# A decode step on one core: the query weights in two loads by partitions, and one gather of x

## Chip, cores and metric

The kernel runs on one core of a Trainium2 chip. The metric is device time in microseconds, the median of several executions. Times inside the kernel come from one execution recorded by the hardware profiler; they count from the first instruction (the start of the span).

## What is computed

Two token rows x (B = 2, D = 448, bfloat16) are normalised and go through two branches, attention against a cache and a small feed-forward net, whose results are multiplied:

```python
def reference(A_x, A_k_cache, A_v_cache, A_wq, A_wo, B_x, B_w1, B_w2):
    def _A_ref(x, k_cache, v_cache, wq, wo):          # Hq=16, Hkv=8, Dh=256
        ...
        W = min(4096, max(256, Sk // 4))              # Sk=8192, W=2048: the last 2048 keys
        q = (x @ wq).reshape(B, Sq, Hq, Dh).transpose(0, 2, 1, 3)
        k = jnp.repeat(k_cache[:, :, Sk - W:, :], rep, axis=1)
        v = jnp.repeat(v_cache[:, :, Sk - W:, :], rep, axis=1)
        scores = jnp.einsum("bhqd,bhkd->bhqk", q, k) * (Dh ** -0.5)
        o = jnp.einsum("bhqk,bhkd->bhqd", _softmax(scores, axis=-1), v)
        return o.transpose(0, 2, 1, 3).reshape(B, Sq, Hq * Dh) @ wo
    def _B_ref(x, w1, w2):
        h = jnp.maximum(jnp.einsum("bsd,df->bsf", x, w1), 0)      # Dff=1792
        return jnp.einsum("bsf,fd->bsd", h, w2)
    xn = _layernorm(A_x, axis=-1)
    return A_x + _A_ref(xn, ...) * _silu(_B_ref(xn, B_w1, B_w2))
```

The inputs that weigh are the K and V windows (16.8 MB each), wq and wo (3.67 MB each) and w1 and w2 (1.6 MB each).

## The kernel before

The program lists each engine's instructions by hand (`pr.op`, `pr.dma`), in order, with the instructions each depends on; a helper turns these into semaphore waits. Each engine works through its own list in order. All large loads are issued by SP, one after the other, and stand in one DMA queue. Nearly all matmuls pass through one helper, so the profile puts them on its line, L383, and all DMAs on L46; tile names tell them apart.

The order of SP's loads: wq in two parts (L297, into `wbuf`), then K of quarter 0 and 1 (`kbuf`), V of quarter 0 (`vbuf`), and later, each behind the work that frees its buffer, K of quarter 2 (waits for the transposes of quarter 0), V 1 (for the P·V matmuls of quarter 0), K 3, V 2, then w1 and w2 into `wbuf` (after the q matmuls), V 3, and wo in four parts into `kbuf`. Each quarter of K or V is 4 MB: 128 partitions with 32 KB each.

Work at the start:

- ACT issues two small loads of x (`x_sb`, `x_c`). POOL clears tiles and builds identities and masks, among them `msk` (L303, L304). DVE computes mean and variance (L322, L323), several small mask tiles, the rest of `msk` (L354) and `rstd` (L356).
- `x_rows` (L359) normalises x and spreads it into `xg`; `x_cols` (L366) transposes `xg` into `xt` and multiplies by a mask, which leaves x as columns, seven slots of four columns. Which element of x a partition holds has to fit the way the rows of the weights lie in `wbuf`. A row of wq is taken as two half rows of 2048 columns, 896 half rows in all. In this kernel half rows 0 to 255 go to slots 0 and 1 (two to a partition), half rows 256 to 895 to slots 2 to 6 (five to a partition). The columns for this are `xq` (three row operations, a transpose, four mask multiplications, L377 to L380).
- `do_q` (L386): 28 matmuls of `xq` and `wbuf` into `fbk`; the first eight wait for the first load, the others for the second. DVE scales the result into `qn` and transposes it into `qt`; `do_qbd` (POOL) spreads it into `qbd`.
- A second gather (L542 to L544) puts x into columns in the layout of w1 (seven half rows to a partition), `xr`, which `do_H` uses much later.
- DVE transposes K of quarter 0 (`kt`, L459, four pieces), and PE computes scores from `qbd` and `kt` into `sbk`.

After that the quarters follow each other: maximum, exponential, transpose of the probabilities, P·V into `obk`; the feed-forward net stands before the last quarter's P·V, and the product with wo at the end, in parts as wo lands (`wbk` for the wide columns, `cbk` for the rest).

The listing has the functions that the change touches:

Of the kernel before, what the change touches and what calls it, by code (L numbers as in the profile page):

```python
# [5 lines left out]
BF = mybir.dt.bfloat16  # L6
F32 = mybir.dt.float32
ACT = mybir.ActivationFunctionType
ALU = mybir.AluOpType
AX = mybir.AxisListType  # L10

PE, DVE, ACTE, SP, POOL = "pe", "dve", "act", "sp", "pool"
# [151 lines left out]
def bass_recurrent_scan__sliding_block_cached__dense_activation_relu__decode_kernel(  # L164
# [11 lines left out]
    B, Sq, D = A_x.shape  # L176
# [12 lines left out]
    SLOTS = 7  # L189
    HC = HD // 2  # L190
# [8 lines left out]
    with es:  # L199
        pr = _Prog(nc, es)  # L200

        def named(name, shape, dt):
            return es.enter_context(nc.sbuf_tensor(name, shape, dt))

        def psum(name, shape, dt):
            return es.enter_context(nc.psum_tensor(name, shape, dt))

        def view(t, off, dims, n=128, p0=0, pstep=1):
            width = t.shape[1]
            return bass.AP(t, p0 * width + off, [[width * pstep, n]] + dims)  # L210
# [4 lines left out]
        par8 = named("par8", [128, 8], F32)  # L215
# [8 lines left out]
        x_sb = named("x_sb", [128, D], BF)  # L224
        xg = named("xg", [128, 9 * 128], BF)
        xt = named("xt", [128, SLOTS * 128], BF)
# [2 lines left out]
        sd = named("sd", [128, 3], F32)  # L229
        rstd = named("rstd", [128, 1], F32)  # L230
        xr = named("xr", [128, SLOTS * 4], BF)
        xq = named("xq", [128, SLOTS * 4], BF)
        msk = named("msk", [128, 2 * SLOTS], F32)
        qn = named("qn", [128, 512], BF)
        qt = named("qt", [128, 512], BF)
        qbd = named("qbd", [128, QW], BF)
# [24 lines left out]
        wbuf = named("wbuf", [128, SLOTS * HC], BF)  # L261
# [6 lines left out]
        fbk = psum("fbk", [128, 512], F32)  # L268
# [5 lines left out]
        def kv_src(k, cache):  # L274
            return cache.rearrange("b h s d -> (b h) s d")[k::NQ, SK - W:SK, :].rearrange("g (i t) d -> i g (t d)", t=NT)

        st = {}
        wq_rows = A_wq.rearrange("r (hf c) -> (r hf) c", hf=2)
        wq_src = [wq_rows[0:256, :].rearrange("(p s) c -> p (s c)", s=2),
                  wq_rows[256:896, :].rearrange("(p s) c -> p (s c)", s=5)]  # L280
        w1_src = B_w1.rearrange("r (hf c) -> (r hf) c", hf=2).rearrange("(p s) c -> p (s c)", s=SLOTS)
        w2_src = B_w2.rearrange("(p j) n -> p (j n)", j=14)
        wo_src = A_wo.rearrange("(p j) n -> p (j n)", j=32)
# [2 lines left out]
        def load_k(k):  # L286
            d_k[k] = pr.dma(SP, kbuf[k % 2][:, :], kv_src(k, A_k_cache), [st.get(("T", k - 2, 3))])

        def load_v(k):
# [4 lines left out]
        p_xz = pr.op(POOL, lambda e: e.memset(xg[0:32, :], 0.0))  # L294
        d_xc = pr.dma(ACTE, view(x_c, 0, [[1, NCOL]], n=8, pstep=16),
                      A_x[:, 0, :].rearrange("b (i n) -> i b n", i=4), [p_xc], key="v")
        d_wq = [pr.dma(SP, wbuf[:, lo * HC:hi * HC], src) for lo, hi, src in ((0, 2, wq_src[0]), (2, SLOTS, wq_src[1]))]  # L297
        load_k(0)
        load_k(1)
        load_v(0)  # L300

        i0 = pr.op(POOL, lambda e: e.memset(ident[:, :], 0.0))
        p_m0 = pr.op(POOL, lambda e: e.memset(msk[:, 0:4], 0.0))  # L303
        p_m1 = pr.op(POOL, lambda e: e.memset(view(msk, 0, [[3, 2]]), 1.0), [p_m0])  # L304
        p_id = pr.op(POOL, lambda e: e.affine_select(
            out=ident[:, :], in_=ident[:, :], compare_op=ALU.not_equal, fill=1.0,
            base=0, pattern=[[-1, 128]], channel_multiplier=1), [i0])
# [3 lines left out]
            out=ident_f[:, :], in_=ident_f[:, :], compare_op=ALU.not_equal, fill=1.0,  # L311
            base=0, pattern=[[-1, 128]], channel_multiplier=1), [i1])
        for t0 in (h_sb, h_n, ea, ga):
            p_z = pr.op(POOL, lambda e, t0=t0: e.memset(t0[:, :], 0.0))
        p_one = pr.op(POOL, lambda e: e.memset(one_f[:, :], 1.0))
        p_sz = pr.op(POOL, lambda e: e.memset(sel[:, :], 0.0))

        a_z = [pr.op(ACTE, lambda e, t=t: e.memzero(t[:, :]), key="osb" if t is obk else None)
               for t in (fbk, obk, wbk, cbk)]

        v_xz = p_xz
# [3 lines left out]
            out=sd[0:B, 0:1], in0=st2[0:B, 1:2], scalar1=EPS, scalar2=None, op0=ALU.add), [v_ag])  # L325
# [3 lines left out]
            out=par2[:, :], in_=view(ident, 0, [[1, 2], [2, 64]]), axis=AX.X, op=ALU.add), [p_id])  # L329
        v_par8 = pr.op(DVE, lambda e: e.tensor_copy(  # L330
            view(par8, 0, [[2, 4], [1, 2]]), view(par2, 0, [[0, 4], [1, 2]])), [v_par])
# [3 lines left out]
            out=view(wcol, 0, [[4, 128], [1, 4]], n=4), in0=view(ident, 0, [[0, 128], [1, 4]], n=4),  # L335
            scalar1=1.0, scalar2=BIG, op0=ALU.subtract, op1=ALU.mult))
        v_qm = pr.op(DVE, lambda e: e.tensor_reduce(
            out=qmask[:, :], in_=view(ident, 0, [[32, 4], [1, 32]]), axis=AX.X, op=ALU.add))
# [6 lines left out]
        def fold8_op(e):  # L345
# [4 lines left out]
            view(gsum, 0, [[8, 16], [1, 8]]), view(fold8, 0, [[0, 16], [1, 8]])), [v_f8])  # L350
        v_sz = p_sz
        v_sel = pr.op(DVE, lambda e: e.tensor_copy(view(sel, 0, [[16, 2]]), fold[:, 0:2]), [v_fold, v_sz], key="pt")
        v_m1 = p_m1
        v_m2 = pr.op(DVE, lambda e: e.tensor_copy(  # L354
            view(msk, 4, [[2, 5], [1, 2]]), view(par8, 0, [[1, 5], [1, 2]])), [v_par8])
        v_rs = pr.op(DVE, lambda e: e.reciprocal(rstd[0:B, :], sd[0:B, 1:2]), [a_sd])  # L356
        xs = {"deps": [v_rs, v_xz], "mask": [v_m1, v_m2]}

        def x_rows(lo, blocks, pairs, step, shift, first, behind=False):  # L359
            xs["xn"] = pr.op(DVE, lambda e: e.tensor_scalar(  # L360
                out=view(xg, 128 + 128 * lo + shift, [[256, blocks], [128, 2], [pairs, 128 // pairs]], n=B),
                in0=view(x_sb, first, [[1, blocks], [0, 2], [step, 128 // pairs]], n=B),
                scalar1=st2[0:B, 0:1], scalar2=rstd[0:B, 0:1],
                op0=ALU.subtract, op1=ALU.mult), xs["deps"] + ([xs["xn"]] if behind else []))

        def x_cols(dst, mask):  # L366
            v = pr.op(DVE, lambda e: e.transpose(xt[0:32, :], xg[0:32, 128:128 + SLOTS * 128]),
                      [xs["xn"]] + xs.get("done", []))
            for g in range(4):
                o = pr.op(DVE, lambda e, g=g: e.tensor_tensor(  # L370
                    out=view(dst, 0, [[4, SLOTS], [2, 2], [1, 2]], n=32, p0=32 * g),
                    in0=view(xt, 32 * g, [[128, SLOTS], [1, 2], [0, 2]], n=32),
                    in1=mask, op=ALU.mult), [v, p_one, a_z[-1]] + xs["mask"])
            xs["deps"], xs["done"] = [v], [o]
            return o

        x_rows(2, 3, 2, 5, 0, 128)  # L377
        x_rows(2, 3, 2, 5, -127, 130)
        x_rows(0, 1, 1, 1, 0, 0, True)
        v_xr = x_cols(xq, view(msk, 0, [[2, SLOTS], [0, 2], [1, 2]], n=32))  # L380

        def mm(out_ap, lhsT, rhs, start, stop=False, **kw):
            return lambda e: e.matmul(out_ap, lhsT=lhsT, rhs=rhs, start=start, stop=stop,  # L383
                                      skip_group_check=True, **kw)

        def do_q():  # L386
            deps = [d_wq[0], v_xr]
            for s in range(SLOTS):
                if s == 2:
                    deps = [d_wq[1]]  # L390
                for i in range(4):
                    lo = s * HC + i * 512
                    o = pr.op(PE, mm(fbk[32 * i:32 * i + 4, :], xq[:, 4 * s:4 * s + 4], wbuf[:, lo:lo + 512],
                                     s == 0, s == SLOTS - 1, tile_position=(0, 32 * i)), deps)
                    deps = []
            st["q_mm"] = o
            v = pr.op(DVE, lambda e: e.tensor_scalar(  # L397
                out=view(qn, 0, [[64, 8], [32, 2], [1, 32]]),
                in0=view(fbk, 0, [[64, 8], [1, 2], [2, 32]]),
                scalar1=SCALE, scalar2=None, op0=ALU.mult), [o])  # L400
            st["qT"] = pr.op(DVE, lambda e: e.transpose(qt[:, :], qn[:, :]), [v])
# [7 lines left out]
                deps = []  # L409

        def do_H(u):
            deps = [d_w1, v_xw] if u == 0 else []
            for s in range(SLOTS):
                lo = s * FC + u * (FC // 2)
                o = pr.op(PE, mm((fbk, cbk)[u][0:4, 0:FC // 2], xr[:, 4 * s:4 * s + 4], wbuf[:, lo:lo + FC // 2],
                                 s == 0, s == SLOTS - 1), deps)
                deps = []
            st["h_n"] = pr.op(DVE, lambda e: e.tensor_scalar(
                out=view(h_n, 32 * u, [[64, 14], [1, 32]], n=4), in0=view((fbk, cbk)[u], 0, [[1, 14], [14, 32]], n=4),
                scalar1=0.0, scalar2=None, op0=ALU.max), [o, p_z])  # L420
# [117 lines left out]

        pr.section("PRO", 0)
        do_q()  # L540
        do_qbd(0)
        x_rows(0, 4, 2, SLOTS, -127, 3)  # L542
        x_rows(0, 4, 2, SLOTS, 0, 0)
        v_xw = x_cols(xr, view(par8, 0, [[1, SLOTS], [0, 2], [1, 2]], n=32))  # L544
        for c in range(4):
            do_T(0, c)
        do_S(0, 0)
# [13 lines left out]
        for k in range(1, NQ):  # L561
# [9 lines left out]
            if k == 2:  # L571
                d_w1 = pr.dma(SP, wbuf[:, 0:W2], w1_src, [st["q_mm"]])
# [35 lines left out]
        deps = [st["at", NQ - 1]]  # L608
        for b in range(2):
            m_at = pr.op(PE, mm(mbk[:, 256 + 32 * b:288 + 32 * b], at_exp[:, 128 * b:128 * b + 128],  # L610
                                fold[:, :], b == 0, b == 1), deps)
            deps = []
        keep_busy(sbk, 512)
        v_at2 = pr.op(DVE, lambda e: e.tensor_copy(at2[:, :], mbk[:, 256:320]), [m_at])
        deps = [v_at2]
        for j in range(WO_WIDE):
            i = j % 4
            m_w = pr.op(PE, mm(wbk[32 * i:32 * i + 2, 0:D], view(at2, j, [[32, 2]]), wo_sb[:, j * D:(j + 1) * D],
                               j < 4, j + 4 >= WO_WIDE, tile_position=(0, 32 * i)), deps + [landed.get(j)])
            deps = []  # L620
# [11 lines left out]
        deps = [v_ws]  # L632
        for i in range(4):
            pr.op(PE, mm(cbk[32 * i:32 * i + 17, 0:NCOL], sel[:, :], wsum[:, i * NCOL:(i + 1) * NCOL],
                         True, tile_position=(0, 32 * i)), deps)
            deps = []
        for j in range(WO_WIDE, 32):
# [4 lines left out]
            out=tmp[:, :], in0=cbk[:, 0:NCOL], in1=g_sb[:, :], op=ALU.mult), [m_o, st["g"]])  # L642
        v_o = pr.op(DVE, lambda e: e.tensor_tensor(
            out=out_sb[:, :], in0=tmp[:, :], in1=x_c[:, :], op=ALU.add), [v_t, d_xc])
# [33 lines left out]
```

## Time and profile before

| | |
|---|---|
| median of three runs | 109.77 us (109.68 to 109.82) |
| profiled execution | 109.78 us |
| its span, first to last instruction | 108.5 us |
| PE / PEld / DVE / ACT / POOL busy | 70.5 / 27.2 / 60.5 / 14.9 / 9.0 us |
| mean granted TensorE clock | 0.900 |
| bytes moved, mean rate | 44.13 MB, 407 GB/s |
| issue to landing, first and second part of wq | 4.9 and 10.6 us |

An engine's busy time is no sign of being the bound by itself; what counts is which wait ended last before each step. A time from issue to landing includes the time that a load stands behind others in the queue. KB is 1024 bytes, MB and GB are powers of ten.

### The profile page before, as it was taken

Reading aid. Unit: us, or ns where it says so; the run is one execution under the profiler, and the core shown is the slowest. Engines: PE = TensorE matmul, PEld = TensorE weight load, DVE = VectorE, ACT = ScalarE, POOL = GpSimd, SP = SyncE. Lnnn points to the kernel's source line nnn. Section 1 sums busy time; section 2 is a strip of 40 time slices with the busy share of each in tenths; the row PEclk is TensorE's granted clock in tenths of the full one; section 3 lists DMA queues with packets and bytes.
Section 4 is the critical chain, followed back from the end, with each engine's and each line's share of the span. In section 5 each row is a group of like instructions: output and inputs, shape, how many; then the busy total and the mean of one; then the engine's idle time right before and its main releaser. Section 6 shows DMA issues by size and latency. Waiting matters only on the chain.

```text
span 108.5 us, 1111 instructions
## 1 busy us (share of the span) xinstructions
PE 70.5 (65%) x424; PEld 27.2 (25%) x424; DVE 60.5 (56%) x86; ACT 14.9 (14%) x33; POOL 9.0 (8%) x35
## 2 busy tenths in 40 slices
PE   0000940019994999994999994729859689596651
PEld 0000200003341533342333342313223244142220
DVE  0589078099924999406999304499910435605122
ACT  2991000000000300010300020300002030017000
POOL 7900023000003000003000003000000000000000
PEclk9999999999999556999755999855899999999997
DMA  2999998899899998999899988999899998999970
GB/s 60 448 439 408 483 483 387 387 471 495 387 387 411 532 411 387 411 483 459 387 399 459 496 387 387 411 544 399 387 379 440 523 423 387 411 394 436 399 294 7
DMA packets 2333, 44.13 MB, mean 407 GB/s; under 512 B 282, under 2 KB 412, under 8 KB 668
## 3 DMA queue, kind: packets, MB, share of 16 engines
q1 hardware_dynamic: 2304, 44.11, 95.3%
q8 instruction: 1, 0.02, 0.1%
q10 hardware_dynamic: 28, 0.01, 0.0%
HBM read 44.11 MB, written 0.00 MB: 407 GB/s over the span
## 4 chain that ended last, share of the span: by engine, by line
DMA 67%; PE 24%; DVE 4%; SPq 2%; issue 1%; DVEq 0%
DMA vbuf<-in_A_v_cache_dram 29%; DMA kbuf<-in_A_wo_dram 19%; DMA kbuf<-in_A_k_cache_dram 18%; PE sbk L383 14%; PE obk L383 5%; DVE kt L459 2%; PE wbk L491 2%; SPq L46 2%; PE cbk L383 1%; DVE rm L506 1%; DVE wsum L621 1%; PE wbk L383 1%; PE mbk L383 0%; DVE mx L515 0%; DVE tmp L641 0%
## 5 line engine op out<-in xcount | busy, mean ns | idle before, releaser
L383 PE MATMUL sbk<-kt,qbd 128*128 128x512 bf16 x128 | 38.1, 463 | 12.0 <-DVE kt L459 12.0
L459 DVE STREAM_TRANSPOSE kt<-kbuf 128x2048 f32<-128x2048 f32 x16 | 35.7, 2274 | 3.1 <-DMA kbuf<-in_A_k_cache_dram 3.1
L383 PEld LDWEIGHTS sbk<-kt,qbd 128*128 128x128 bf16 x128 | 13.9, 113 | 35.8 <-issue 27.5
L506 DVE TENSOR_REDUCE rm<-sbk 128x1 f32<-128x512 f32 x4 | 2.8, 692 | 19.7 <-PE nbk L383 16.6
L383 PE MATMUL fbk<-wbuf,xq 128*4 128x512 bf16 x28 | 3.2, 620 | 11.0 <-DVE xq L370 11.0
L406 POOL COPY qbd<-qt 32x64 bf16<-32x64 bf16 x16 | 4.5, 282 | 57.2 <-PE sbk L383 46.4
L383 PE MATMUL obk<-vbuf,pt 128*16 128x512 bf16 x128 | 7.6, 379 | 1.9 <-DMA vbuf<-in_A_v_cache_dram 1.6
L487 ACT ACTIVATE o_sb<-obk,rs 128x512 bf16<-128x512 f32 x4 | 2.8, 688 | 31.6 <-PE obk L383 31.6
L523 ACT ACTIVATE bias<-mbk 128x1 f32<-128x1 f32 x4 | 0.7, 171 | 42.3 <-PE mbk L383 42.3
L491 PE MATMUL wbk<-ident_f 128*128 128x512 f32 x8 | 5.4, 766 | 0.0
L530 DVE STREAM_TRANSPOSE pt<-e_sb 128x512 bf16<-128x512 bf16 x4 | 2.7, 684 | 3.2 <-ACT e_sb L524 3.2
L383 PEld LDWEIGHTS obk<-vbuf,pt 128*16 128x16 bf16 x128 | 2.8, 89 | 6.5 <-DMA vbuf<-in_A_v_cache_dram 3.3
L383 PEld LDWEIGHTS fbk<-wbuf,xq 128*4 128x4 bf16 x28 | 0.7, 101 | 12.5 <-issue 11.8
L383 PE MATMUL fbk<-wbuf,h_sb 128*17 128x448 bf16 x14 | 2.8, 352 | 1.4 <-DVE h_sb L427 1.4
L383 PE MATMUL mbk<-one_f,mrow 1*128 1x1 f32 x8 | 1.5, 256 | 2.8 <-DVE mrow L518 2.8
L510 PE MATMUL mbk<-ident_f,rm 128*1 128x128 f32 x4 | 1.1, 270 | 3.2 <-DVE rm L506 3.2
L360 DVE TENSOR_SCALAR xg<-x_sb,st,rstd 2x384 bf16<-2x384 bf16 (+2 forms) x5 | 2.8, 600 | 0.1
L524 ACT ACTIVATE e_sb<-sbk,bias 128x512 bf16<-128x512 f32 x4 | 2.8, 688 | 0.4
L621 DVE COPY wsum<-wbk 128x448 f32<-128x448 f32 x1 | 0.6, 625 | 3.7 <-PE wbk L383 3.7
L322 DVE BATCH_NORM_STATS2 st<-x_sb 2x6 f32<-2x448 bf16 x1 | 0.6, 616 | 3.7 <-DMA x_sb<-in_A_x_dram 3.7
L383 PEld LDWEIGHTS nbk<-ssum,gsum 128*128 128x128 f32 x8 | 1.7, 250 | 3.8 <-ACT e_sb L524 3.4
L397 DVE TENSOR_SCALAR qn<-fbk 128x512 bf16<-128x512 f32 x1 | 0.7, 693 | 3.4 <-PE fbk L383 3.4
(85 smaller groups left out, 52.4 us busy)
## 6 DMA issues: line engine op xcount, KB each, us to landing
kbuf<-in_A_k_cache_dram SPq DMA_DIRECT2D x4, 4096.0 KB, 21.9
vbuf<-in_A_v_cache_dram SPq DMA_DIRECT2D x4, 4096.0 KB
wbuf<-in_B_w_dram SPq DMA_DIRECT2D x2, 1568.0 KB, 22.2
wbuf<-in_A_wq_dram SPq DMA_DIRECT2D x1, 2560.0 KB, 10.6
kbuf<-in_A_wo_dram SPq DMA_DIRECT2D x1, 2240.0 KB, 20.0
wbuf<-in_A_wq_dram SPq DMA_DIRECT2D x1, 1024.0 KB, 4.9
kbuf<-in_A_wo_dram SPq DMA_DIRECT2D x1, 672.0 KB, 21.1
kbuf<-in_A_wo_dram SPq DMA_DIRECT2D x1, 448.0 KB, 21.7
```

The source lines that it names most:

```text
L46: o = _Op(eng, lambda e: e.dma_start(dst, src), deps, True, key)
L360: xs["xn"] = pr.op(DVE, lambda e: e.tensor_scalar(out=view(xg, 128 + 128 * lo + shift, [[256, blocks], [128, 2], [pairs, 128 // pairs]], n=B),
L383: return lambda e: e.matmul(out_ap, lhsT=lhsT, rhs=rhs, start=start, stop=stop, skip_group_check=True, **kw)
L406: st["qbd", k] = pr.op(POOL, lambda e, a=a: e.tensor_copy(view(qbd, 24 + 32 * a, [[128, 8], [2, 4], [1, 2]], n=32, p0=32 * a), view(qt, 0, ...
L459: st["T", k, c] = pr.op(DVE, lambda e: e.transpose(view(dst, 32 * c, [[128, NT], [1, 32]]), view(src, 32 * c, [[128, NT], [1, 32]])), deps ...
L487: st["osb", k] = pr.op(ACTE, lambda e: e.activation(o_sb[:, :], obk[:, :], ACT.Copy, scale=rs[:, k:k + 1]), [st["PV", k], st["rs", k]], ke ...
L491: pr.op(PE, lambda e: e.matmul(bank[:, 0:n], lhsT=ident_f[:, :], rhs=view(ident_f, 0, [[0, n // 128], [1, 128]]), start=True, stop=True))
L506: st["rm", k] = pr.op(DVE, lambda e: e.tensor_reduce(out=rm[:, :], in_=sbk[:, :], axis=AX.X, op=ALU.max), [st["S", k, 7]], key="rm")
L510: st["rmT", k] = pr.op(PE, lambda e: e.matmul(mbk[0:1, 0:128], lhsT=rm[:, :], rhs=ident_f[:, :], start=True, stop=True, is_transpose=True) ...
L524: st["exp", k] = pr.op(ACTE, lambda e: e.activation(e_sb[:, :], sbk[:, :], ACT.Exp, bias=bias[:, 0:1], accum_out=ssum[:, 0:1]), [a], key=" ...
L530: st["pt", k] = pr.op(DVE, lambda e: e.transpose(pt[:, :], e_sb[:, :]), [st["exp", k]], key="pt")
L621: v_ws = pr.op(DVE, lambda e: e.tensor_copy(wsum[:, :], wbk[:, 0:D]), [m_w])
```

## The change

wq gets the layout of w1: seven half rows to a partition, 28 KB. It comes in two loads by partitions: partitions 0 to 15 first, then 16 to 127. Both weights then ask for the same columns of x, so there is one gather, into `xr`, used by `do_q` and `do_H`; `xq`, `msk` and the second gather go. `do_q` waits for both loads ahead of its first matmul.

```diff
-        xq = named("xq", [128, SLOTS * 4], BF)
-        msk = named("msk", [128, 2 * SLOTS], F32)
...
-        wq_rows = A_wq.rearrange("r (hf c) -> (r hf) c", hf=2)
-        wq_src = [wq_rows[0:256, :].rearrange("(p s) c -> p (s c)", s=2),
-                  wq_rows[256:896, :].rearrange("(p s) c -> p (s c)", s=5)]
+        wq_src = A_wq.rearrange("r (hf c) -> (r hf) c", hf=2).rearrange("(p s) c -> p (s c)", s=SLOTS)
...
-        d_wq = [pr.dma(SP, wbuf[:, lo * HC:hi * HC], src) for lo, hi, src in ((0, 2, wq_src[0]), (2, SLOTS, wq_src[1]))]
+        d_wq = [pr.dma(SP, wbuf[lo:hi, :], wq_src[lo:hi, :]) for lo, hi in ((0, 16), (16, 128))]
...
-        p_m0 = pr.op(POOL, lambda e: e.memset(msk[:, 0:4], 0.0))
-        p_m1 = pr.op(POOL, lambda e: e.memset(view(msk, 0, [[3, 2]]), 1.0), [p_m0])
...
-        v_m2 = pr.op(DVE, lambda e: e.tensor_copy(
-            view(msk, 4, [[2, 5], [1, 2]]), view(par8, 0, [[1, 5], [1, 2]])), [v_par8])
...
-        x_rows(2, 3, 2, 5, 0, 128)
-        x_rows(2, 3, 2, 5, -127, 130)
-        x_rows(0, 1, 1, 1, 0, 0, True)
-        v_xr = x_cols(xq, view(msk, 0, [[2, SLOTS], [0, 2], [1, 2]], n=32))
+        for shift, first in ((-127, 3), (0, 0)):
+            v_xn = pr.op(DVE, lambda e, shift=shift, first=first: e.tensor_scalar(
+                out=view(xg, 128 + shift, [[256, 4], [128, 2], [2, 64]], n=B),
+                in0=view(x_sb, first, [[1, 4], [0, 2], [SLOTS, 64]], n=B),
+                scalar1=st2[0:B, 0:1], scalar2=rstd[0:B, 0:1],
+                op0=ALU.subtract, op1=ALU.mult), [v_rs, v_xz])
+        v_xt = pr.op(DVE, lambda e: e.transpose(xt[0:32, :], xg[0:32, 128:128 + SLOTS * 128]), [v_xn])
+        for g in range(4):
+            v_xr = pr.op(DVE, lambda e, g=g: e.tensor_tensor(
+                out=view(xr, 0, [[4, SLOTS], [2, 2], [1, 2]], n=32, p0=32 * g),
+                in0=view(xt, 32 * g, [[128, SLOTS], [1, 2], [0, 2]], n=32),
+                in1=view(par8, 0, [[1, SLOTS], [0, 2], [1, 2]], n=32), op=ALU.mult), [v_xt, p_one, a_z[-1], v_par8])
...
         def do_q():
-            deps = [d_wq[0], v_xr]
+            deps = d_wq + [v_xr]
             for s in range(SLOTS):
-                if s == 2:
-                    deps = [d_wq[1]]
                 for i in range(4):
                     lo = s * HC + i * 512
-                    o = pr.op(PE, mm(fbk[32 * i:32 * i + 4, :], xq[:, 4 * s:4 * s + 4], wbuf[:, lo:lo + 512],
+                    o = pr.op(PE, mm(fbk[32 * i:32 * i + 4, :], xr[:, 4 * s:4 * s + 4], wbuf[:, lo:lo + 512],
...
         def do_H(u):
-            deps = [d_w1, v_xw] if u == 0 else []
+            deps = [d_w1] if u == 0 else []
...
         do_qbd(0)
-        x_rows(0, 4, 2, SLOTS, -127, 3)
-        x_rows(0, 4, 2, SLOTS, 0, 0)
-        v_xw = x_cols(xr, view(par8, 0, [[1, SLOTS], [0, 2], [1, 2]], n=32))
```

More of the change, by code (lines that the diff above doesn't have):

```diff
@@ L352, in bass_recurrent_scan__sliding_block_cached__dense_activation_relu__decode_kernel @@
         v_sel = pr.op(DVE, lambda e: e.tensor_copy(view(sel, 0, [[16, 2]]), fold[:, 0:2]), [v_fold, v_sz], key="pt")
-        v_m1 = p_m1
-        v_m2 = pr.op(DVE, lambda e: e.tensor_copy(
-            view(msk, 4, [[2, 5], [1, 2]]), view(par8, 0, [[1, 5], [1, 2]])), [v_par8])
         v_rs = pr.op(DVE, lambda e: e.reciprocal(rstd[0:B, :], sd[0:B, 1:2]), [a_sd])
[L357 to L362, printed above, removed]
-                scalar1=st2[0:B, 0:1], scalar2=rstd[0:B, 0:1],
-                op0=ALU.subtract, op1=ALU.mult), xs["deps"] + ([xs["xn"]] if behind else []))
@@ L366, in x_cols @@
[L366 to L375, printed above, removed]
```

## The prediction

> **What bounds the kernel now.** I read the chain of waits first, in order of time, then the DMA share of the span by windows, then the start of the timeline, because the change touches only the first two loads and the work that consumes them. The chain (start, duration, what; times are microseconds from the start of the span):
>
> ```profile
> 1.64 19.83 DMA kbuf<-in_A_k_cache_dram
> ...
> 21.56 2.32 DVE kt L459
> ...
> 24.02 9.47 PE sbk L383 x32
> ...
> 45.88 14.46 DMA vbuf<-in_A_v_cache_dram
> ...
> 62.34 17.46 DMA vbuf<-in_A_v_cache_dram
> ...
> 83.01 21.08 DMA kbuf<-in_A_wo_dram
> ...
> 104.14 0.56 PE wbk L383 x6
> ...
> 106.47 0.28 DVE out_sb L643
> ```
>
> Four pieces of this chain are loads of 14 to 21 us, counted from issue to landing. Most of such a time is standing in the queue, as the next view shows. Its columns are the window, its length, busy time of PE, PEld, DVE, ACT and POOL, the granted clock, the mean busy share of the 16 DMA engines, and GB/s. A load is counted in the window in which its packets start, so a short window can read above 1.
>
> ```profile
> 1.75:2.00 0.25, 0.00 (x0) 0.00 (x0) 0.00 (x0) 0.00 (x0) 0.25 (x2) 1.00 1.80 262
> 2.00:2.25 0.25, 0.00 (x0) 0.00 (x0) 0.00 (x0) 0.12 (x1) 0.19 (x3) 1.00 0.20 66
> 2.25:2.50 0.25, 0.00 (x0) 0.00 (x0) 0.00 (x0) 0.25 (x1) 0.16 (x2) 1.00 0.34 98
> 2.50:2.75 0.25, 0.00 (x0) 0.00 (x0) 0.00 (x0) 0.25 (x1) 0.25 (x2) 1.00 0.77 229
> 2.75:3.00 0.25, 0.00 (x0) 0.00 (x0) 0.00 (x0) 0.25 (x1) 0.25 (x1) 1.00 0.76 302
> 3.00:3.50 0.50, 0.00 (x0) 0.00 (x0) 0.00 (x0) 0.49 (x2) 0.50 (x2) 1.00 1.09 459
> 12.00:104.00 92.00, 68.19 (x378) 26.38 (x370) 52.87 (x61) 8.57 (x24) 4.51 (x16) 0.89 1.00 429
> ```
>
> From 12 to 104 us the engines of the DMA are busy the whole time (share 1.00) at 429 GB/s. PE and DVE have gaps, the DMA has none. So the kernel is one long queue of loads, with a start of about 1.75 us before the first packet and a tail of about 4.4 us (104.09, where the chain's last load lands, to 108.5, the end of the span). Whatever holds the queue up early is never made good: with no idle stretch behind it, each microsecond lost by all 16 engines in the loads of wq comes out as a microsecond at the end. Whatever lies beside the queue, as long as it keeps its distance, costs nothing. The page of the profile opens with the span:
>
> ```profile
> span 108.5 us, 1111 instructions
> ```
>
> The profiled execution took 109.78, so 1.28 us lie around the span, and the median of the runs is 109.77. I add to 109.78 and carry the result over as it is.
>
> **Part one: the loads of wq.** The same 3.5 MB come first in the queue in both kernels, in two DMAs of SP. Before:
>
> ```profile
> 0.74 0.85 SPq L46 DMA_DIRECT2D wbuf<-in_A_wq_dram  x2
> ```
> ```profile
> wbuf<-in_A_wq_dram SPq DMA_DIRECT2D x1, 2560.0 KB, 10.6
> ...
> wbuf<-in_A_wq_dram SPq DMA_DIRECT2D x1, 1024.0 KB, 4.9
> ```
> ```profile
> q1 hardware_dynamic: 2304, 44.11, 95.3%
> ```
>
> Both loads reach all 128 partitions: 128 rows of 8 KB, then 128 of 20 KB. After, the first reaches partitions 0 to 15 with rows of 28 KB (448 KB, 0.459 MB), the second partitions 16 to 127 (3136 KB, 3.211 MB). Sixteen rows are one for each engine, 112 are seven, so by count every engine still moves 28 KB eight times. The issues stay two, at 0.85 us for both; nothing on SP moves past anything else. There are 128 packets fewer of 2304. The q1 row gives 0.953 x 108.5 x 16 = 1654 engine-microseconds for them, 0.72 us each on average, nearly all of it bytes; what a packet costs beside its bytes no row separates. If it were as much as 10% of the mean, 0.07 us, eight packets fewer on each engine would save 0.6 us; I take nothing.
>
> The real question is whether 16 neighbouring partitions take data as fast as 128 do. No load of before shows that: every large one goes to all 128. The nearest rows bound it. At one end partitions don't matter: 0.459 MB at 429 GB/s is 1.07 us, the same share of the queue as before, a cost of 0. At the other end a partition takes no more than it takes on average in the long window, 429 / 128 = 3.35 GB/s. A row of 28,672 bytes then needs 8.55 us, 7.48 us more than 1.07. All 16 engines have such a row first, so all lose that. Between these ends stands the number of separate ways that lead into the 16 partitions: 16 ways cost 0; eight 1.07 us; four 4 x 1.07 = 4.28 us, so 3.21 more; two 7.48. I take four ways, +3.2 us, the case closest to the middle of the two ends (3.74), because the nearest row is the long window with eight partitions to an engine, which points to few ways rather than to sixteen, yet says nothing of which partitions share one.
>
> [...]
>
> The second load, 112 rows, takes 3.211 MB / 429 = 7.49 us if it spreads evenly. It leaves the ways of partitions 0 to 15 less used, so the others carry eight rows where an engine moves seven: the fullest way needs 8 x 28,672 bytes at 429 / 16 = 26.8 GB/s, 8.55 us, 1.07 more. Where engines also run into each other on one way, it is more: if half the rows are moved at half speed, the 7.49 us become 11.2, +3.7. I take 0 in the sum, since the first load's wait also staggers the engines, and keep +1.1 to +3.7 for a rival.
>
> A gain is bounded too. In the five windows from 1.75 to 3.00 the queue moved 0.25 x (262 + 66 + 98 + 229 + 302) = 239 KB, where 429 GB/s would have moved 536. The missing 297 KB are 0.69 us of the queue. A first DMA of one row for each engine might be handed out sooner and close that gap: -0.7 us at most. I take 0 for this in the sum.
>
> **Part two: x into columns once.** The chain of before up to q, and the second gather behind it:
>
> ```profile
> 2.00 0.09 POOL L303 MEMSET msk<- 128x4 f32 x1
> 2.15 0.10 POOL L304 MEMSET msk<- 128x2 f32 x1
> ...
> 6.55 0.16 DVE L354 COPY msk<-par 128x10 f32<-128x10 f32 x1
> ...
> 7.21 1.67 DVE L360 TENSOR_SCALAR xg<-x_sb,st,rstd 2x384 bf16<-2x384 bf16 x3
> ...
> 8.92 1.10 DVE L367 STREAM_TRANSPOSE xt<-xg 32x896 bf16<-32x896 bf16 x1
> ...
> 10.05 0.75 DVE L370 TENSOR_TENSOR xq<-xt,msk 32x28 bf16<-32x28 bf16 x4
> ...
> 10.95 3.16 PE L383 MATMUL fbk<-wbuf,xq 128*4 128x512 bf16 x28 [10.95 <-DVE xq L370]
> ...
> 11.79 0.11 PEld L383 LDWEIGHTS fbk<-wbuf,xq 128*4 128x4 bf16 x8 [0.74 <-DMA wbuf<-in_A_wq_dram]
> ...
> 14.16 0.69 DVE L397 TENSOR_SCALAR qn<-fbk 128x512 bf16<-128x512 f32 x1 [3.35 <-PE fbk L383]
> 14.88 0.71 DVE L401 STREAM_TRANSPOSE qt<-qn 128x512 bf16<-128x512 bf16 x1
> 15.52 1.21 DVE L360 TENSOR_SCALAR xg<-x_sb,st,rstd 2x512 bf16<-2x512 bf16 x2
> 15.66 1.75 POOL L406 COPY qbd<-qt 32x64 bf16<-32x64 bf16 x4 [10.32 <-DVE qt L401]
> 16.77 1.10 DVE L367 STREAM_TRANSPOSE xt<-xg 32x896 bf16<-32x896 bf16 x1
> 17.90 0.75 DVE L370 TENSOR_TENSOR xr<-xt,par 32x28 bf16<-32x28 bf16 x4
> ```
>
> On POOL two memsets go (0.19 us), on DVE the copy into msk (0.16), the first gather's three row operations (1.67) are replaced by two of the other shape (1.21), and the second gather, 15.52 to 18.65, goes whole. The columns are then ready at about 7.21 + 1.21 + 1.10 + 0.75 = 10.3, half a microsecond earlier, and wait for wq in any case. None of these 3.7 us is on the chain: DVE next has the transpose of kt, which waits for the load of K until 21.56. Their worth is 0.
>
> What gets worse is q. Before, 8 of 28 matmuls ran ahead of the second landing; after 11.79 the other 20 took until 14.11, 0.116 us each. After the change all 28 wait for both loads, 28 x 0.116 = 3.25 us from the landing instead of 2.32, so q comes 0.93 us later. Behind the waiting matmul stands only the one that opens the scores; behind qn on DVE stands kt. If the landing stays at 11.79, qt ends at 15.59 + 0.93 = 16.5, 5 us before kt may start at 21.56, and qbd ends at 17.41 + 0.93 = 18.3, 5.7 us before the scores start at 24.02. If the loads of wq are late by some microseconds, K, next in the same queue, is late by the same amount, and the distances stay. So this costs 0; without that cover it would cost 0.93.
>
> **Sum.** Loads +3.2, second load 0, start 0, packets 0, x 0, q 0: 109.78 + 3.2 = 113.0 us.
>
> **The rivals.** A difference of 0.2% (0.22 us) is about what a measurement of this kernel tells from none; the three runs lie within 0.14 us.
>
> First, the forecast: the 16 rows crowd, the second load spreads about evenly. The DMA share of 1.00 behind it speaks for a full pass to the end; that no row shows a narrow load speaks against certainty. Slower by 0.3 to 4.3 us (one term of 1.07 on either side of 3.2, and fewer ways shared), centre 113.0. Chance 0.50.
>
> Second, both loads crowd: 3.2 plus 1.1 to 3.7, or two ways at 7.5: 114.1 to 117.3, centre 116. For it: the uneven remainder of 112 partitions follows from the same cause. Against: the staggering. Chance 0.24.
>
> Third, on the other side: partitions don't matter, and the one-row DMA fills the hole between 1.75 and 3.00 us. Its price is -0.7 at most, half of it -0.35: 109.1 to 109.5. It decides only if the 16 rows take less than 1.07 + 0.69 = 1.76 us, since above that the crowding eats the whole hole. For it: those five windows hold the one visible loss of the queue. Against: the hole may be the first answer of memory, which any first row waits for. Chance 0.17.
>
> Fourth, the change does nothing that counts: the bytes, the two issues and the eight rows for each engine are the same, x was beside the queue. 109.6 to 110.0. Chance 0.09.
>
> **How the numbers follow.** Forecast 113.0. The slower cases hold 0.50 + 0.24 = 0.74, faster 0.17, same 0.09. The range runs from 109.3, the middle of the third rival, to 117.3, the bound of two ways; about 0.08 lie below and 0.06 above. The likeliest side alone is 110.1 to 117.3.
>
> **What would show it.** In the profile of after, the DMA row of the first slices and windows from 2 to 7 us should show about a quarter of 429 GB/s, near 107, until about 6 us, then the old rate; the load of 448 KB should land about 5 to 6 us after its issue rather than about 3; K should land near 24.7 instead of 21.47, and every later piece of the chain should be shifted by the same amount, with the tail from the last wide matmuls unchanged. No wait for qbd should appear ahead of the first scores. The prediction is wrong if K lands within 0.3 us of 21.47 (third or fourth), if it lands beyond 26 (second), or if K shifts and the end doesn't.

## The result, and the profile after

The changed kernel takes 117.52 us, median of five runs (116.91 to 117.80), against 109.77 before: 1.0675 times as long, 95% interval 1.0635 to 1.0716. The profiled execution took 116.96 us with a span of 115.6 us, 7.18 and 7.1 more than before; the sums below are made against these. Forecast were 113.0 us and a range to 117.3: the sign was right, but the forecast +3.2 is less than half of what was measured, which lies just beyond the range.

The chain of waits after, the pieces that answer to those shown of before:

```profile
1.64 27.14 DMA kbuf<-in_A_k_cache_dram
...
28.88 2.32 DVE kt L437
...
31.33 9.89 PE sbk L363 x32
...
51.94 15.69 DMA vbuf<-in_A_v_cache_dram
...
69.62 17.44 DMA vbuf<-in_A_v_cache_dram
...
90.27 21.03 DMA kbuf<-in_A_wo_dram
...
111.34 0.56 PE wbk L363 x6
...
113.64 0.27 DVE out_sb L618
```

The chain has the same members. K of the first quarter lands at 1.64 + 27.14 = 28.78 instead of 21.47, 7.31 us later; the second part of wo, which lets the last wide matmuls go, lands at 111.30 instead of 104.09, 7.21 later. So the whole loss is there when the first K lands, and nothing of it is made good or added in the 82 us that follow. The landing of K is the measure for all experiments below: in the queue it stands directly behind the loads of wq.

The windows of after (last two columns: busy share of the 16 DMA engines, GB/s):

```profile
4.00:6.00 2.00, 0.00 (x0) 0.00 (x0) 0.00 (x0) 1.98 (x5) 1.28 (x7) 1.00 1.25 230
6.00:8.00 2.00, 0.00 (x0) 0.00 (x0) 1.12 (x4) 0.96 (x2) 0.00 (x0) 1.00 0.96 229
8.00:12.00 4.00, 0.00 (x0) 0.00 (x0) 3.88 (x12) 1.50 (x3) 0.00 (x0) 1.00 0.78 237
12.00:16.00 4.00, 0.00 (x0) 0.00 (x0) 0.78 (x5) 0.00 (x0) 0.00 (x0) 1.00 1.22 308
16.00:20.00 4.00, 0.74 (x8) 0.27 (x12) 0.00 (x0) 0.00 (x0) 0.00 (x0) 1.00 0.85 291
20.00:28.00 8.00, 2.95 (x25) 0.66 (x17) 1.40 (x2) 0.00 (x0) 0.95 (x4) 1.00 1.03 442
28.00:100.00 72.00, 55.96 (x281) 22.26 (x281) 44.38 (x41) 5.86 (x15) 2.88 (x12) 0.88 1.00 431
```

Two things stand in the first five rows. The engines of the DMA are as busy as ever (about 1 on average), but they move 229 to 308 GB/s, so a packet takes longer on average. From 4 to 6 us that is 1.25 x 16 engines x 2 us over the 16 rows of 28 KB that 230 GB/s make, 2.5 us for a row; at 429 GB/s a row takes an engine 1.07 us. And the low rate lasts long past the first load. Where the two loads land says the same:

```profile
wbuf<-in_A_wq_dram SPq DMA_DIRECT2D x1, 3136.0 KB, 18.0
...
wbuf<-in_A_wq_dram SPq DMA_DIRECT2D x1, 448.0 KB, 5.9
```

The 16 rows land 5.9 us after their issue, the 112 rows twelve later, where 3.211 MB at the old rate need 7.5. From 20 us on the rate is the old one. Of the signs that the prediction named, the landing of the 448 KB came as foretold (5 to 6 us after its issue). The rate did not: it was to be near 107 GB/s until about 6 us and then the old one. And K beyond 26 us was its own sign for the second rival, that both loads crowd.

### The profile page after: what moved, and what is told of

Read it like the earlier page. It is cut to its first block, busy times and chain, and to the rows that moved or that the text cites. A ratio compares the mean times of both kernels' runs of the same rounds, so it can differ in the third digit from the quotient of the medians.

```text
span 115.6 us, 1099 instructions
## 1 busy us (share of the span) xinstructions
PE 69.3 (60%) x424; PEld 27.0 (23%) x424; DVE 57.0 (49%) x77; ACT 14.9 (13%) x33; POOL 8.2 (7%) x33
## 4 chain that ended last, share of the span: by engine, by line
DMA 70%; PE 21%; DVE 4%; SPq 2%; issue 1%; DVEq 0%
DMA vbuf<-in_A_v_cache_dram 29%; DMA kbuf<-in_A_k_cache_dram 23%; DMA kbuf<-in_A_wo_dram 18%; PE sbk L363 13%; PE obk L363 5%; DVE kt L437 2%; SPq L46 2%; PE wbk L469 1%; DVE rm L484 1%; PE cbk L363 1%; DVE wsum L596 1%; PE wbk L363 0%; PE mbk L363 0%; DVE mx L493 0%; DVE tmp L616 0%
## 5 line engine op out<-in xcount | busy, mean ns | idle before, releaser
L363 PE MATMUL sbk<-kt,qbd 128*128 128x512 bf16 x128 | 36.6, 448 | 11.7 <-DVE kt L437 11.7
L363 PEld LDWEIGHTS sbk<-kt,qbd 128*128 128x128 bf16 x128 | 13.4, 109 | 34.2 <-issue 24.3
L363 PE MATMUL fbk<-wbuf,xr 128*4 128x512 bf16 (+1 forms) x35 | 5.5, 600 | 19.3 <-DMA wbuf<-in_A_wq_dram 19.3
L363 PE MATMUL obk<-vbuf,pt 128*16 128x512 bf16 x128 | 8.2, 379 | 3.1 <-DMA vbuf<-in_A_v_cache_dram 3.1
L384 POOL COPY qbd<-qt 32x64 bf16<-32x64 bf16 x16 | 3.8, 240 | 65.2 <-PE sbk L363 46.0
L363 PEld LDWEIGHTS fbk<-wbuf,xr 128*4 128x4 bf16 x35 | 1.5, 113 | 21.9 <-issue 21.9
L419 ACT ACTIVATE ea<-fbk 17x112 f32<-17x112 f32 x4 | 1.0, 253 | 9.8 <-PE fbk L363 9.7
L469 PE MATMUL sbk<-ident_f 128*128 128x512 f32 x4 | 2.2, 639 | 0.0
```

The source lines that it names most:

```text
L384: st["qbd", k] = pr.op(POOL, lambda e, a=a: e.tensor_copy(view(qbd, 24 + 32 * a, [[128, 8], [2, 4], [1, 2]], n=32, p0=32 * a), view(qt, 0, ...
L419: a_e = pr.op(ACTE, lambda e, i=i: e.activation(ea[32 * i:32 * i + 17, :], fbk[0:17, i * NCOL:(i + 1) * NCOL], ACT.Exp, scale=-1.0), [st[" ...
L469: pr.op(PE, lambda e: e.matmul(bank[:, 0:n], lhsT=ident_f[:, :], rhs=view(ident_f, 0, [[0, n // 128], [1, 128]]), start=True, stop=True))
```

## The experiments

All are variants of the changed kernel. Theory A says that a load to some of the 128 partitions goes at the rate of the ways that lead to them; its rivals put the cost on the long rows, the layout of the source, or the one gather of x. one_load, cols_2_5 and one_load_5 were timed over several runs; every other experiment is one run with its trace.

**One load to all partitions.** The change without its split:

```diff
-... for lo, hi in ((0, 16), (16, 128))]
+... for lo, hi in ((0, 128),)]
```

> The changed kernel with wq in one load to all 128 partitions (rows of 28 KB as in the change, one gather of x). Theory A, few partitions take data more slowly: the whole loss is gone, K lands at 21.2 to 21.6 us and the time is 109.5 to 110.0. Theory B, rows of 28 KB or the missing head start of q cost the time, whatever the partitions: 115 or more. Theory C, the one gather of x is late: K lands as before but the first scores wait for qbd, 110.5 or more.

Measured: 109.93 us, ratio to before 0.9991 (0.9954 to 1.0029). The chain's piece for K:

```profile
1.17 20.40 DMA kbuf<-in_A_k_cache_dram
```

K lands at 21.57. The whole loss is gone with the split; rows of 28 KB (B) and the one gather (C) cost nothing that can be measured. This kernel is the base of what follows: each extra load stands ahead of its single load of wq and goes to a spare tile that nothing reads, so what K's landing moves beyond 21.57 is the price of that load. Two traces of this kernel (one_load and one_load_5) have K at 21.57 and 21.68, so a difference of 0.1 us says nothing. The span of every kernel below is longer than that of the base (108.4 us) by the same price, within 0.2 us.

```diff
+        spare = named("spare", [128, SLOTS * HC], BF)
+        d_ex = pr.dma(SP, spare[0:16, :], wq_src[0:16, :])
-        d_wq = [pr.dma(SP, ...
+        d_wq = [d_ex] + [pr.dma(SP, ...
```

**The 16 rows by themselves**, to neighbouring partitions and to every eighth one (`view(spare, 0, [[1, SLOTS * HC]], n=16, pstep=8)`):

> As one_load, with one more load ahead of it: 16 rows of 28 KB into partitions 0 to 15 of a spare tile that nothing reads (448 KB more; q waits for it too). At 429 GB/s they cost 1.07 us. Theory A with four ways: 4.3 us more than one_load, K at about 25.8. If the 16 rows alone made the whole loss of 7.75 us of the change: 8.8 us more than one_load, K at about 30.3. Theory B: 1.1 more.

> As ex16_next, the same 16 rows of the source, but into partitions 0, 8, 16 to 120 of the spare tile. Theory A, the destination's partitions decide: 1.1 to 2.2 us more than one_load (as many ways as rows, or half), less than ex16_next by 2 us or more. Theory D, sixteen such rows of the source are slow wherever they go: the same as ex16_next.

K's pieces, first of the neighbours, then of every eighth partition:

```profile
1.63 23.24 DMA kbuf<-in_A_k_cache_dram
```
```profile
2.01 21.37 DMA kbuf<-in_A_k_cache_dram
```

K at 24.87 and 23.38: the 16 rows cost 3.30 us at neighbouring partitions and 1.81 at spread ones, with the same source. The destination decides; theory D falls. Of the 3.30, 1.07 are the bytes, so the first load of the split loses 2.2 us, not the whole 7.2. Theory A had given 4.3 us for the neighbours and 2 us or more between the two; measured are 3.30 and a difference of 1.5. A part of the 16 rows' time is covered: they land 6.0 us after their issue (at about 6.7 us), and from 4 to 6 us rows of the load behind already start at 230 GB/s.

**The 112 rows by themselves**, and the same from another source:

```diff
+        d_ex = pr.dma(SP, spare[16:128, :], wq_src[16:128, :])
```
```diff
+        d_ex = pr.dma(SP, spare[16:128, :], A_k_cache[0, 0].rearrange("(p t) d -> p (t d)", t=64)[16:128, 0:14336])
```

> As one_load, with one more load ahead of it: 112 rows of 28 KB into partitions 16 to 127 of a spare tile that nothing reads (3136 KB more). Spread evenly at 429 GB/s it costs 7.5 us more than one_load. If the 112 rows crowd by themselves, as the second load of the change (landing at about 18 us, 12 us after the first) suggests: 11 to 13 us more. If they crowd only behind a staggered first load: 7.5 to 8.6.

> As ex112, the extra 112 rows of 28 KB into partitions 16 to 127 of the spare tile, but read from the K cache with a pitch of 32 KB between rows instead of 28 KB. Theory A, the destination decides: 13 us more than one_load, as ex112 (13.4). Theory D, the layout of the source decides: 7.5 to 9 us more.

K's piece and one window with the 112 rows of wq, then K's piece with those of the K cache:

```profile
1.65 33.32 DMA kbuf<-in_A_k_cache_dram
```
```profile
8.00:12.00 4.00, 0.00 (x0) 0.00 (x0) 3.86 (x13) 1.36 (x2) 0.00 (x0) 1.00 1.02 251
```
```profile
1.64 33.71 DMA kbuf<-in_A_k_cache_dram
```

K at 34.97 and 35.35: 13.4 and 13.8 us for bytes that need 7.5. The 112 rows are slow with no narrow load ahead of them, and from a source with another pitch. In the window above a row takes 1.02 x 16 x 4 us over the 35 rows that 251 GB/s make, 1.9 us instead of 1.07. The 112 rows lose 5.9 us; with the 2.2 of the 16 rows that makes 8.1, of which the change shows 7.2, 0.9 less than the sum.

**The control**, the same 3136 KB in 128 rows (`spare[:, 0:12544]`):

> As ex112, with the same 3136 KB of wq in the extra load, but in 128 rows of 24.5 KB over all partitions. Control: at 429 GB/s 7.5 us more than one_load; theory A says 7.3 to 7.7. If an extra load ahead of wq costs more than its bytes for another reason: 9 us more or beyond.

```profile
1.64 27.56 DMA kbuf<-in_A_k_cache_dram
```

K at 29.20, 7.63 us where the bytes take 7.49 at 429 GB/s: beyond them the extra load as such cost 0.14 us, hardly more than the 0.1 between two traces.

**Other order**, `((16, 128), (0, 16))`:

> The changed kernel with its two loads in the opposite order, partitions 16 to 127 first, then 0 to 15. If each load has its own price (3.4 us for the 16 rows, about 5.9 more than its even 7.5 for the 112), or the two share it by running into each other, the sum stays near that of the change: K at 28 to 31 us, 117 to 119. If the 112 rows are slow only because the 16 rows ahead stagger the engines: K below 26, under 114.

```profile
1.64 28.76 DMA kbuf<-in_A_k_cache_dram
```

K at 30.40, 8.83 us later than with one load, 118.66 us in the one run. That is 0.7 more than the 8.1 of the two alone, where the change has 0.9 less. So both loads cost in either order, the 112 rows also with nothing ahead of them, and the order moves the sum by 1.6 us; no run shows why.

**Two halves, and even and odd partitions.** Both have two loads of 64 rows:

```diff
+... for lo, hi in ((0, 64), (64, 128))]
```
```diff
+        d_wq = [pr.dma(SP, view(wbuf, 0, [[1, SLOTS * HC]], n=64, p0=lo, pstep=2), wq_src[lo::2, :]) for lo in (0, 1)]
```

> The changed kernel with wq in two loads of 64 partitions, 0 to 63 and 64 to 127, rows of 28 KB. 64 rows are four for each engine and start on whole groups of four. Theory A, the ways into the destination: if 64 neighbouring partitions reach half of the ways, both loads run at half the rate, 8.5 us become 17, K lands near 29.9, 8.5 us later than with one load, and the time is 118.3. Theory E, what hurts is only that 16 and 112 rows do not fall on whole groups: K near 21.6, 110 us.

> The changed kernel with wq in two loads of 64 rows of 28 KB, the even partitions first, then the odd ones: each load reaches from one end of the 128 partitions to the other. Theory F, a load runs at full rate if its partitions reach all over the 128: K near 21.6 us, 110 us. Theory G, the number of rows decides how they are dealt to the engines, and any number but 128 lets engines meet on a way: as with the two halves, K at 29.5 to 31, 118 to 119.5.

A window and K's piece of the halves, then of even and odd:

```profile
8.00:12.00 4.00, 0.00 (x0) 0.00 (x0) 2.29 (x6) 0.49 (x2) 0.00 (x0) 1.00 1.10 230
```
```profile
1.99 28.82 DMA kbuf<-in_A_k_cache_dram
```
```profile
8.00:12.00 4.00, 0.00 (x0) 0.00 (x0) 2.28 (x6) 0.49 (x2) 0.00 (x0) 1.00 1.09 468
```
```profile
1.97 19.90 DMA kbuf<-in_A_k_cache_dram
```

The halves run at 230 GB/s, about half of the full rate (2.2 us for a row, worked out as above, against 1.07 for even and odd), and K lands at 30.81 (+9.24). Even and odd partitions run at full rate, K at 21.87 (+0.30), 110.19 us in the one run. Same rows, same bytes, same number of loads: which partitions one load reaches makes 9 us of difference. Theory E, whole groups, falls with the halves; theory G, the number of rows alone, with even and odd. Theory F holds for these two, but the 16 rows at every eighth partition reach from end to end too and cost 1.7 times their bytes. The rows of wq that one load reads change along with the partitions here and in the next loads; only the two pairs above, with the same 16 rows of the source and with 112 rows of another source, keep the two apart, and both speak for the destination.

**Reach or number of rows.** Extra loads of 64 rows at partitions 0 to 63 and 32 to 95, of 96 rows at 32 to 127, of 112 rows at 0 to 111:

> As one_load, with an extra load of 64 rows of 28 KB (1792 KB) into partitions 0 to 63 of the spare tile ahead of it; at 429 GB/s it costs 4.28 us. Half the rate, as both halves of wq suggest: K lands 8.0 to 9.0 us later than with one load. If only two such loads in a row are slow: 4.3 to 5.

> As ex64_low, into partitions 32 to 95. Theory H, the ways are those of the two halves, 0 to 63 and 64 to 127, so that 64 rows across the middle reach all of them: 4.3 to 5.3 us. Theory I, any 64 neighbouring partitions share half of the ways: 8 to 9, as ex64_low.

> As ex64_low, 96 rows (2688 KB) into partitions 32 to 127, six for each engine; 6.42 us at 429 GB/s. If the number of rows decides (each engine's run of rows crosses the borders of the ways and meets its neighbour's, as with 112): 10 to 13 us. If 112 is slow because of its seven rows, an odd number, alone: 6.4 to 7.5.

> As ex112, 112 rows into partitions 0 to 111 instead of 16 to 127. If the number of rows decides: 13 to 14 us as ex112 (13.4). If the start at partition 16 decides: 7.5 to 9.

K's pieces, in this order, one kernel to a fence:

```profile
1.98 28.58 DMA kbuf<-in_A_k_cache_dram
```
```profile
2.02 24.44 DMA kbuf<-in_A_k_cache_dram
```
```profile
1.66 33.12 DMA kbuf<-in_A_k_cache_dram
```
```profile
1.66 32.56 DMA kbuf<-in_A_k_cache_dram
```

| extra load | MB | K lands, us | price, us | at 429 GB/s, us | price over that |
|---|---|---|---|---|---|
| 16 rows, 0 to 15 | 0.459 | 24.87 | 3.30 | 1.07 | 3.1 |
| 16 rows, every eighth | 0.459 | 23.38 | 1.81 | 1.07 | 1.7 |
| 64 rows, 0 to 63 | 1.835 | 30.56 | 8.99 | 4.28 | 2.1 |
| 64 rows, 32 to 95 | 1.835 | 26.46 | 4.89 | 4.28 | 1.1 |
| 96 rows, 32 to 127 | 2.753 | 34.78 | 13.21 | 6.42 | 2.1 |
| 112 rows, 0 to 111 | 3.211 | 34.22 | 12.65 | 7.49 | 1.7 |
| 112 rows, 16 to 127 | 3.211 | 34.97 | 13.40 | 7.49 | 1.8 |
| 128 rows, all (24.5 KB) | 3.211 | 29.20 | 7.63 | 7.49 | 1.0 |

Sixty-four neighbouring partitions are at half rate from 0 (2.1 times the price of the bytes) and at nearly full rate from 32, across the middle (1.1 times): theory H holds, I falls. That is what separate ways into the two halves of the 128 would give, a load inside one half using half of them, and the 230 GB/s of the two halves of wq agree; the ways themselves stand in no view of the profile. The 16 rows cost 3.1 times their bytes, less than the four times that four ways of 16 would make, so the prediction's number four is not shown.

Reach alone doesn't explain the loads of 96 and 112 rows, though: all three reach partitions of both halves and still cost 1.7 to 2.1 times their bytes. That neighbouring engines meet on one way with 96 and 112 rows, as ex96 supposed, was not shown: which engine takes which row stands in no view of the profile, and even and odd partitions, 64 rows to a load at +0.30 us, speak against any simple rule of this kind. So why these loads are slow stays open: theory A, reach alone, explains the loads of 64 rows and not these.

**A better version?** One gather of x with the old split by slots (rows of 8 and 20 KB to all partitions), and one load again:

```diff
+        d_wq = [pr.dma(SP, wbuf[:, lo * HC:hi * HC], wq_src[:, lo * HC:hi * HC]) for lo, hi in ((0, 2), (2, SLOTS))]
```

> The changed kernel (one gather of x) with wq again in two loads to all 128 partitions, slots 0 and 1, then slots 2 to 6: rows of 8 KB and 20 KB, read from the same 28 KB rows. Theory A: as before, 109.5 to 110.0, no difference above 0.2%, since the second gather of before lay beside the loads. If the shorter first rows start the queue later than rows of 28 KB: up to 0.4 us more than one_load.

> one_load again, timed in more rounds: within 0.2% of before, 109.5 to 110.0. The start of the queue in one_load moved 344 GB/s between 1.75 and 3.00 us where before moved 191 on average, which would be worth up to 0.4 us if it carried through; the single run of each profile shows K landing 0.1 us later, not earlier, so the expectation is 0 to -0.2 us.

Measured: 109.74 us, ratio 0.9987 (0.9962 to 1.0012), and 109.85 us, ratio 0.9984 (0.9956 to 1.0011). Neither can be told from before; they are simpler, not faster.

## Why the prediction was wrong

**What bounds the kernel**: right. This queue, busy from 28 to 100 us at a share of 1.00, handed the early loss on to the end: 7.31 us at the first K, 7.21 at wo.

**The first load, +3.2**: that 16 neighbouring partitions take data more slowly was right; the size was 1.0 us too large. Measured alone it is 3.30 with its bytes, so +2.2: 3.1 times the bytes, where four ways would make 4 times. The four was the author's estimate; no run shows a number of ways.

**The second load, 0**: this step failed. It measured +5.9 alone and about 5 in the change (7.2 less the 2.2 of the first), more than the +3.2 that the whole forecast was made of. The prediction named the crowding but took 0 because "the first load's wait also staggers the engines"; the 112 rows lose no less with nothing ahead of them, and no run shows the staggering. Its upper bound, 3.7, was too low as well: it let half of the rows go at half speed, which is 1.5 times the bytes, where the price was 1.8 times. No row of before ruled out all rows at half speed, +7.5, and with that bound the range would have held the result. An equal count of rows for each engine (seven instead of eight) was taken for spreading evenly, and the 112 rows alone cost 13.40 us instead of 7.49. What makes the 112 rows slow stays open.

**The rivals.** The second, both loads crowd, is what happened: its centre is 1.5 us below the 117.52 measured. That its bound, 117.3, comes so near is luck, since it stands for 16 rows on two ways (+7.5), which cost 2.2. The first was said to reach one term of 1.07 to either side of 3.2, which is 2.1 to 4.3, not 0.3 to 4.3; the range doesn't hang on it. The third failed at its own condition: the 16 rows took 3.30 us, not under 1.76. And longer first rows don't close the hole at the start, as one_load shows, whose rows are all of 28 KB and go to all partitions:

```profile
1.75:3.00 1.25, 0.00 (x0) 0.00 (x0) 0.00 (x0) 0.88 (x1) 1.01 (x4) 1.00 1.28 344
...
8.00:12.00 4.00, 0.09 (x4) 0.10 (x8) 3.21 (x10) 0.48 (x2) 0.00 (x0) 1.00 0.99 425
```

It starts 344 GB/s between 1.75 and 3.00 us where before has 191, and K lands no sooner (21.57 against 21.47). A row is counted where it starts (after reads 1491 GB/s from 1.75 to 2.00 us and 0 from 2.50 to 4.00), so longer rows put more bytes into these windows. But the first rows take 1.28 x 16 x 1.25 us over 15 rows, 1.7 us each, against 1.07 from 8 us on: one_load loses about 0.6 us at its start too, close to the 0.69 of before. That fits what the prediction held against this rival, that any first row waits. The fourth fails with the loss.

**Packets, 0**: right within what can be measured; one_load has the long rows and the time of before.

**x and q, 0**: right. The work of after ahead of the scores:

```profile
6.79 0.61 DVE L316 BATCH_NORM_STATS2 st<-x_sb 2x6 f32<-2x448 bf16 x1 [6.79 <-DMA x_sb<-in_A_x_dram]
...
12.11 0.75 DVE L357 TENSOR_TENSOR xr<-xt,par 32x28 bf16<-32x28 bf16 x4
...
19.26 3.15 PE L363 MATMUL fbk<-wbuf,xr 128*4 128x512 bf16 x28 [19.26 <-DMA wbuf<-in_A_wq_dram]
...
22.46 0.69 DVE L375 TENSOR_SCALAR qn<-fbk 128x512 bf16<-128x512 f32 x1 [9.61 <-PE fbk L363]
23.19 0.71 DVE L379 STREAM_TRANSPOSE qt<-qn 128x512 bf16<-128x512 bf16 x1
23.97 1.08 POOL L384 COPY qbd<-qt 32x64 bf16<-32x64 bf16 x4 [18.69 <-DVE qt L379]
28.88 4.50 DVE L437 STREAM_TRANSPOSE kt<-kbuf 128x2048 f32<-128x2048 f32 x2 [4.97 <-DMA kbuf<-in_A_k_cache_dram]
```

From the landing of wq (19.23) to the start of qn are 3.23 us, 0.86 more than before's 2.37 after its second landing; 0.93 were forecast. The distance from qt to kt is 4.97 us, as forecast (5). The columns of x were not early: x itself comes to DVE at 6.79 instead of 3.70, and the columns stand at 12.86 where 10.3 were forecast. The slow rows alone don't explain this: DVE's first work, the one on x, starts at about 5.3 us in one_load, whose rows run at full rate (0.68 us of it lie between 5 and 6), and at about 2.3 with the two halves, whose rows are slow (0.70 us between 1.75 and 3.00). No run isolated the cause. As the columns still wait 6 us for wq, it costs nothing.

## What to carry to other kernels

In this queue, which never idles (share 1.00 from 28 to 100 us), the price of a load was its share of the queue, and a load to some of the 128 partitions cost up to 3.1 times its bytes (the 16 neighbouring rows) while the engines showed as busy as ever (about 1 at 229 to 308 GB/s, where the full rate is 429): read GB/s beside the busy share, and the landing of the first load behind it. Where a weight is split, try columns (109.74 us here) rather than partitions (117.52); if it must be by partitions, even and odd ones were nearly free here (+0.30 us), and the two halves cost 9.24 us. And price each half of a split with its own bound: the harmless-looking remainder, 112 of 128 rows, carried about two thirds of the loss.

## What the runs showed of the hardware beyond that

The four copies into qbd on POOL took 1.75 us before, one of them up to 0.593 us, and take 1.08 us after (the median over all sixteen copies is 0.24 us each in both). In before they ran while DVE worked on the second gather, in after beside an idle DVE; in one_load, which has no second gather either, they take 1.07 us. No run isolated the cause. Loads of 64 rows at partitions 0 to 63 and at 32 to 95 have the same packets and bytes, yet cost 8.99 against 4.89 us: where the tile began made 4.10 us here, and 64 or 112 rows from partition 0 made 3.66 (8.99 against 12.65).
